# Moving the last load of wo behind the last values in the transfer queue of a decode kernel

## The chip, the cores and the metric

The kernel runs on one core of a Trainium2 chip. The metric is the device time of one execution in microseconds (us), shorter is better. Engines are called TensorE (PE in the profile; its weight loads are PEld), VectorE (DVE), ScalarE (ACT), GpSimd (POOL) and SyncE (SP, which issues nearly all transfers here). The granted clock is the share of full speed at which TensorE was allowed to run in a stretch, as the profile records it; 1.00 is full speed.

## The reference, cut to what matters

One new token passes through an attention block with cached keys and values and then a small MLP:

```python
# x: 1 x 640; 32 heads of 192; 32768 cached positions; bf16
q = layernorm(x) @ wq
p = softmax(q . k_cache * 192**-0.5)          # per head, over 32768 positions
h = x + concat(p @ v_cache) @ wo              # wo: 6144 x 640
h2 = h + relu(layernorm(h) @ w1) @ w2         # w1: 640 x 1536, w2: 1536 x 640
```

The two caches are 805 MB. All else together is some 20 MB.

## The kernel before

All loads from memory go through one queue, filled by SyncE in program order. A head's keys come in two loads (6144 KB each), its values in three. `kt` holds keys, `va` and `vb` hold values, `wo_s` holds the three rows per partition of wo that two heads need. Head 31, the last (`LAST`), is cut finer so that less work is left after its last byte: keys k0 to k5, values v0, v1, two halves `vh` and four pieces `vc`.

```python
def load(dst, src, sem, *label):
    g.do(lambda: nc.sync.dma_start(out=dst, in_=src), sem, label, by=16)
...
for h in range(LAST):
    keys(h, 0)
    vals(h, 0)
    keys(h, 1)
    for ld in ((2, 1) if h == 0 else (1, 2)):
        vals(h, ld)
    if h % 2 == 0:
        if h > 0:
            g.wait("prj", h)          # the pair before has been projected
        load(wo_s[:], wo_view[h // 2], "dwo", "wo", h // 2)
...
end_keys(0, 0, JL, "dk0")                                # k0, after waits for head 30
end_values(0, 0, JL * Dh, "dvb", "v", LAST, 0)           # v0
end_keys(1, P * JL, JL, "dke0")                          # k1
...                                                      # k2 to k5, v1, vh, vc
g.wait("PV", LAST, 3)
load(w1_s, B_w1.rearrange("(c p) n -> p c n", p=P), "dw1", "w1")
for i, (c0, c1) in enumerate(zip(W2_CUTS[:-1], W2_CUTS[1:])):    # cuts 0, 6, 9, 11, 12
    load(w2_s[:, c0:c1], B_w2.rearrange("(c p) n -> p c n", p=P)[:, c0:c1], f"dw2_{i}", "w2", i)
```

w1 and w2 go where k0 and k1 were. GpSimd passes landings on to TensorE and VectorE (`relay`), so that a wait for a key or value load reads as a wait for POOLq in the profile. TensorE and ScalarE take somewhat more than half of the keys (transposes, copies, scores as matmuls), VectorE the rest; TensorE does all values. The order of TensorE in head 31:

```python
transposes(g, h, 0); transposes(g, h, 1); scores_pe(g, h, 0)     # k0
values(g, h, 0); scores_pe(g, h, 1)
transposes(g, h, 2)                                              # k1
o_turn(g, h - 1); values(g, h, 1); scores_pe(g, h, 2)
transposes(g, h, 3); transposes(g, h, 4)                         # the latter: k2
...
project(g, h + 1)                                                # waits for the last wo
... h1 = w1 (60 matmuls), then per piece of w2:
for i, (f0, f1) in enumerate(zip(W2_CUTS[:-1], W2_CUTS[1:])):
    g.wait("w2", i)
    pe_group(g, [... w2_s[:, f, n * P:(n + 1) * P] ... for f in range(f0, f1) for n in range(DT)], ("y", i), "pe_dve")
```

The softmax here doesn't subtract the row's maximum and nothing guards it: scores larger than these inputs give would overflow.

## Time and profile before

| | before |
|---|---|
| time, first three runs | 1918.17 us median (1917.4 to 1920.89) |
| span of the profiled execution | 1915.3 us |
| bytes moved, mean rate | 825.29 MB, 431 GB/s |
| landing of k1, issue to landing | 27.7 us |

In a profile line such as those below, the first number is the start in us from the beginning of the span, the second the duration, then engine, source line, operation, what it writes and reads, and how many instructions were merged into the line. What stands in brackets is the idle time of the engine just before, and what ended it. A transfer's line in the list of issues has its size and the time from its issue to its landing. The prediction below shows the lines of before and reads them.

### The profile page before, as it was taken

To read this page: it belongs to the slowest core of one execution; us is meant where nothing else is said; L and a number is where in the kernel's file an instruction comes from. 1 tells how busy PE (TensorE), PEld (TensorE's weight loads), DVE (VectorE), ACT (ScalarE), POOL (GpSimd) and SP (SyncE) were. 2 spreads that over 40 slices of the span, in tenths; PEclk is the share of its full clock that TensorE was granted. 3 is DMA by queue.
4 is the path that set the end of the run, shared out by engine and by line. 5 is a ranking of instruction groups with operands and counts; after the bars stand their busy time and mean duration, and the time that the engine had idled before them with its cause. 6 is when DMAs were issued, how large, how long until landed. Compare 5 with 4: busy or idle time off the path is not lost.

```text
span 1915.3 us, 36109 instructions
## 1 busy us (share of the span) xinstructions
PE 1551.1 (81%) x15899; PEld 1085.0 (57%) x15899; DVE 1561.3 (82%) x731; ACT 939.5 (49%) x2000; POOL 1.0 (0%) x6
## 2 busy tenths in 40 slices
PE   7778887887878788877878877778788787877888
PEld 7555555655555555555556555556555555555555
DVE  2797787987878978789787888878798787987897
ACT  2455454554544544545545445445355454554444
POOL 0000000000000000000000000000000000000000
PEclk9888998888988889888898888898888898888988
DMA  9999999999999999999999999999999999999998
GB/s 409 430 434 433 430 435 431 435 436 433 434 431 434 435 429 431 435 432 439 434 429 435 434 431 435 434 429 437 431 434 438 431 436 429 437 431 433 431 432 367
DMA packets 29650, 825.29 MB, mean 431 GB/s; under 512 B 3131, under 2 KB 4668, under 8 KB 8124
## 3 DMA queue, kind: packets, MB, share of 16 engines
q1 hardware_dynamic: 29616, 824.98, 99.9%
q8 instruction: 15, 0.25, 0.0%
q14 instruction: 7, 0.06, 0.0%
q10 hardware_dynamic: 12, 0.00, 0.0%
HBM read 824.97 MB, written 0.00 MB: 431 GB/s over the span
## 4 chain that ended last, share of the span: by engine, by line
DVE 39%; DMA 38%; PE 15%; ACT 6%; issue 1%; DVEq 0%; POOLq 0%; SPq 0%
DMA kt<-in_A_k_cache_dram 36%; DVE sc L706 19%; DVE pr L703 18%; PE o_ps L360 7%; PE tp L379 6%; ACT kT L606 5%; DMA va<-in_A_v_cache_dram 2%; PE sp L360 1%; DVE o_pair L718 1%; ACT pA L621 1%; DVE oT L728 0%; DMA kt<-in_A_wq_dram 0%; DVE rec L711 0%; DVE rec L712 0%; DVE odd L724 0%
## 5 line engine op out<-in xcount | busy, mean ns | idle before, releaser
L703 DVE TENSOR_TENSOR pr<-kt,qb 128x2304 f32<-128x2304 bf16 (+2 forms) x257 | 756.7, 2944 | 314.8 <-POOLq L321 286.7
L606 ACT COPY kT<-tp 128x1024 bf16<-128x1024 bf16 (+1 forms) x898 | 814.3, 1017 | 272.9 <-PE tp L379 272.9
L379 PE MATMUL tp<-ident_f,kt 128*128 128x128 f32 x3456 | 588.4, 331 | 239.5 <-POOLq L342 162.9
L706 DVE TENSOR_REDUCE sc<-pr 128x12 f32<-128x2304 f32 (+2 forms) x257 | 756.1, 2942 | 8.9
L379 PEld LDWEIGHTS tp<-ident_f,kt 128*128 128x128 f32 x3456 | 482.7, 170 | 291.2 <-POOLq L342 168.7
L360 PE MATMUL o_ps<-va,pB 128*2 128x384 bf16 x1152 | 222.1, 341 | 65.0 <-POOLq L342 65.0
L360 PEld LDWEIGHTS sp<-qm,kT 128*128 128x128 bf16 x6912 | 197.2, 98 | 83.9 <-issue 42.8
L360 PE MATMUL sp<-qm,kT 128*128 128x2 bf16 x6912 | 214.5, 164 | 25.9 <-ACT pB L612 24.4
L360 PE MATMUL o_ps<-vb,pB 128*2 128x384 bf16 x1152 | 213.1, 331 | 22.9 <-ACT pA L621 22.3
L621 ACT ACTIVATE pA<-sc 128x12 bf16<-128x12 f32 (+2 forms) x257 | 58.2, 226 | 346.1 <-DVEq L65 346.1
L612 ACT ACTIVATE pB<-sp 128x20 bf16<-128x20 f32 (+2 forms) x258 | 52.4, 203 | 310.3 <-PE sp L360 310.3
L360 PEld LDWEIGHTS o_ps<-va,pB 128*2 128x2 bf16 x1152 | 94.4, 86 | 161.5 <-POOLq L342 72.4
L360 PE MATMUL o_ps<-va,pA 128*2 128x384 bf16 x896 | 172.2, 334 | 0.0
L360 PE MATMUL o_ps<-vb,pA 128*2 128x384 bf16 x896 | 166.7, 326 | 0.0
L360 PEld LDWEIGHTS o_ps<-vb,pB 128*2 128x2 bf16 x1152 | 89.9, 84 | 122.2 <-ACT pA L621 28.2
L360 PEld LDWEIGHTS o_ps<-va,pA 128*2 128x2 bf16 x896 | 77.4, 86 | 76.1 <-issue 9.6
L360 PEld LDWEIGHTS o_ps<-vb,pA 128*2 128x2 bf16 x896 | 75.2, 84 | 70.2
L612 ACT ACTIVATION_READ_ACCUMULATOR pB<-sp 128x1 f32 x258 | 55.1, 214 | 0.0
L621 ACT ACTIVATION_READ_ACCUMULATOR pA<-sc 128x1 f32 x257 | 53.1, 206 | 0.0
L360 PE MATMUL o_ps<-xn_ln,kt 128*96 128x1 bf16 (+1 forms) x316 | 22.3, 208 | 2.7 <-DMA kt<-in_A_wq_dram 2.7
L360 PEld LDWEIGHTS o_ps<-xn_ln,kt 128*96 128x96 bf16 (+1 forms) x316 | 22.1, 174 | 2.8 <-issue 2.7
L718 DVE TENSOR_SCALAR o_pair<-o_ps,rec 2x384 bf16<-2x384 f32 x32 | 19.4, 605 | 1.5 <-PE o_ps L360 0.4
(69 smaller groups left out, 186.5 us busy)
## 6 DMA issues: line engine op xcount, KB each, us to landing
kt<-in_A_k_cache_dram SPq DMA_DIRECT2D x62, 6144.0 KB, 26.8
vb<-in_A_v_cache_dram SPq DMA_DIRECT2D x63, 3072.0 KB, 20.8
va<-in_A_v_cache_dram SPq DMA_DIRECT2D x31, 6144.0 KB, 26.8
kt<-in_A_k_cache_dram SPq DMA_DIRECT2D x3, 3072.0 KB, 21.3
wo_s<-in_A_wo_dram SPq DMA_DIRECT2D x16, 480.0 KB, 19.0
kt<-in_A_wq_dram SPq DMA_DIRECT2D x4, 1536.0 KB, 10.9
va<-in_A_v_cache_dram SPq DMA_DIRECT2D x1, 3072.0 KB, 30.7
va<-in_A_v_cache_dram SPq DMA_DIRECT2D x2, 1536.0 KB, 35.5
```

Source lines behind the costliest of these rows:

```text
L360: return lambda: pe.matmul(o, lhsT=w, rhs=r, **kw)
L379: calls.append(lambda b=b, o=o: pe.transpose(out=dst[:, b, :], in_=src[:, o:o + 2 * P].bitcast(f32), identity=ident_f[:]))
L606: g.do(lambda: act.copy(out=kT[c % 2][:, b0:b0 + nb, :], in_=src[:, 0:nb, :].bitcast(bf16)), "act_pe", ("cp", h, c, k))
L612: g.do(lambda: act.activation(out=pB[c % NB][:, 0:jp], in_=sp[:, 0:jp], func=F.Exp, scale=SCALE, accum_out=dsums[:, 2 * c + 1:2 * c + 2]), ...
L621: g.do(lambda: act.activation(out=pA[c % NB][:, 0:jd], in_=sc[c % NC][:, 0:jd], func=F.Exp, scale=SCALE, accum_out=dsums[:, 2 * c:2 * c + ...
L703: g.chain(lambda: dve.tensor_tensor(out=pr[:, 0:j1 - j0, :], in0=src[:, (off + j0) * Dh:(off + j1) * Dh].rearrange("p (j d) -> p j d", d=D ...
L706: g.chain(lambda: dve.reduce_sum(out=sc[c % NC][:, j0:j1], in_=pr[:, 0:j1 - j0, :], axis=X), "dve")
L718: g.do(lambda: dve.tensor_scalar_mul(out=o_pair[:, :, 1, :], in0=o_ps[0:2, 0:2 * Dh].rearrange("q (i d) -> q i d", i=2), scalar1=rec[0:2, ...
```

## The change

The last load of wo (for heads 30 and 31) is needed only by the last projection, at the very end, but stands in the queue ahead of all keys and values of head 31. The change puts it behind the last values, so that those keys and values come sooner. The relay of head 30 no longer waits for wo, since the last projection waits for the load itself.

```diff
@@ the queue, heads 0 to 30
-            if h % 2 == 0:
+            if h % 2 == 0 and h < LAST - 1:
                 if h > 0:
                     g.wait("prj", h)
                 load(wo_s[:], wo_view[h // 2], "dwo", "wo", h // 2)
@@ the queue, after head 31's last values
+        g.wait("prj", LAST - 1)
+        load(wo_s[:], wo_view[H // 2 - 1], "dwo", "wo", H // 2 - 1)
         g.wait("PV", LAST, 3)
         load(w1_s, B_w1.rearrange("(c p) n -> p c n", p=P), "dw1", "w1")
@@ relay
-        elif label[1] % 2 == 0:
+        elif label[1] % 2 == 0 and label[1] < LAST - 1:
             g.wait("wo", label[1] // 2)
```

## The prediction

> **What bounds the kernel now.** I read the page first, parts 1, 2 and 4 (busy shares, slices, shares of the chain that ended last), because they say whether the transfers, which are all that the change moves, are the limit.
>
> ```profile
> span 1915.3 us, 36109 instructions
> ...
> DMA  9999999999999999999999999999999999999998
> GB/s 409 430 434 433 430 435 431 435 436 433 434 431 434 435 429 431 435 432 439 434 429 435 434 431 435 434 429 437 431 434 438 431 436 429 437 431 433 431 432 367
> ...
> DVE 39%; DMA 38%; PE 15%; ACT 6%; issue 1%; DVEq 0%; POOLq 0%; SPq 0%
> ```
>
> The DMA rows are full in every slice and move 431 GB/s on average, 825.29 MB in all: for most of the span the kernel is bound by streaming the caches. The change takes no byte away. All that it can win lies at the end, between the place that the last wo load leaves (ahead of head 31's keys) and the place that it takes. So next I read the tail: the issues of transfers in narrow windows, each with its time to landing, which added to the issue time in SyncE's timeline gives when each load is there.
>
> ```profile
> va<-in_A_v_cache_dram SPq DMA_DIRECT2D x1, 6144.0 KB, 26.8
> wo_s<-in_A_wo_dram SPq DMA_DIRECT2D x1, 480.0 KB, 19.0
> kt<-in_A_k_cache_dram SPq DMA_DIRECT2D x1, 3072.0 KB, 16.1
> vb<-in_A_v_cache_dram SPq DMA_DIRECT2D x1, 3072.0 KB, 20.8
> kt<-in_A_k_cache_dram SPq DMA_DIRECT2D x1, 3072.0 KB, 27.7
> ```
>
> By the timeline these were issued at 1814.71 (head 30's last values), 1823.70 (wo), 1833.85 (head 31's first keys, k0), 1836.45 (its first values, v0) and 1836.82 (k1). They land at 1841.5, 1842.7, 1849.95, 1857.25 and 1864.5. The distances are 1.2, 7.25, 7.3 and 7.25 us: one queue, one load after the other, no gap. A 3072 KB piece takes 7.27 us, so the 480 KB of wo take 480/3072 x 7.27 = 1.14 us. Everything behind wo will be there 1.14 us sooner. Then I asked whether anybody waits for it: the chain in order of time, around the landing of k1.
>
> ```profile
> 1836.82 27.69 DMA kt<-in_A_k_cache_dram
> 1864.51 0.02 issue
> 1864.54 0.03 POOLq L342
> 1864.56 0.04 issue
> 1864.61 1.86 PE tp L379 x15
> ```
>
> The chain says that the end hangs on k1, which would promise the whole 1.14 us. But a chain names only the last releaser, not how much later it was than the next one. That is in TensorE's timeline and in the waits of 1855.8 to 1864.7:
>
> ```profile
> 1841.62 3.16 PE L360 MATMUL o_ps<-va,pB 128*2 128x384 bf16 x10 [2.83 <-POOLq L342]
> ...
> 1863.71 0.75 PE L360 MATMUL sp<-qm,kT 128*128 128x2 bf16 x24
> 1864.61 1.86 PE L379 MATMUL tp<-ident_f,kt 128*128 128x128 f32 x15
> ```
>
> ```profile
> PEld tp L379 <- POOLq L342: 0.2, 1, 0.2
> ```
>
> TensorE was at head 31's second group of scores until 1864.46 and took up k1 at 1864.61. It had waited 0.15 us (its weight side 0.23, the 0.2 of the last line). It was last held up for long at 1841.62, by head 30's last values, which are issued ahead of wo in both kernels. From there to the end it works nearly without a break.
>
> **What the Trainium skill says.** "DMA: Bandwidth & Descriptors", section "Queues, rings and completion order": on each DMA engine descriptors are consumed in ring order. The trace agrees: head 30's values land at 1841.5, wo 1.2 us later, k0 7.25 us after that, though wo was issued 10 us ahead of k0. The same page, "Anatomy of one DMA": waits for semaphores are made by the issuing sequencer, the DMA engines only consume their queues. So the moved wait (for head 29's projection) costs the queue nothing: it is long over by about 1874. The same page, "Specifications", gives a fabric ceiling of 435 GB/s and an HBM limit per core of some 358; the trace has 431, so the queue is at the former and past the latter, and no order of loads makes it faster. "TensorE: Matmul & The Clock Gate", section "What's actually happening": the clock is granted by a free-running window of activity of about 3.4 us, whose phase differs from run to run. The trace agrees as far as it can: the granted clock is 0.59 in 1842 to 1846 and 0.50 in 1884 to 1888, and 1.00 in most stretches between. That is a source of scatter larger than the effect.
>
> **The change part by part.**
>
> *Removed ahead of head 31's keys:* one wait, one issue (0.33 us on SyncE, in idle time, with 10 us to the next issue) and 1.14 us of queue. GpSimd's relay for head 30 no longer waits for wo; its next relay waits for k0 anyway, 7 us later. No compute instruction changes: the order of TensorE, VectorE, ScalarE is the same line for line.
>
> *Moved sooner by 1.14 us:* k0 to k5 and all of head 31's values. Their takers:
> - k0 (1849.95 to 1848.8): VectorE takes it at 1850.10 after 1.67 us idle, so it starts 1.1 us sooner and is done with the first chunk at 1855.7 instead of 1856.84. Then it needs the denominator of head 30, which TensorE gives at 1855.84 to 1856.24, from work that the change doesn't reach. So VectorE keeps 1856.99 - 1856.35 = about 0.6 us. Its last scores end at 1900.86 and are used by 1904.40: 3 us of slack, worth nothing.
> - k1 (1864.5 to 1863.4): TensorE gains the 0.15 to 0.23 us that it had waited.
> - k2: TensorE waits 0.55 us for it, until 1872.15, but ScalarE's copies run without idle time from 1870.77 to 1888.4 and set the pace there; an earlier transpose only waits for them. Worth 0.
> - The values: v1 (1855.94 + 30.7 = 1886.6) is used at 1887.23, behind transposes; the last four pieces land at 1896 to 1901.3 and are used at 1899.75 to 1903.0. TensorE is busy without a gap from 1887.2 to 1905.5. Worth 0.
>
> *Added behind the last values:* wo lands where the values ended, at about 1901.3. It is used at 1906.87 (projection): 5.5 us of slack. w1 and w2 keep their landings, for the same bytes lie ahead of them: w1 1894.27 + 11.8 = 1906.1, used at 1908.30; the last piece of w2 at 1911.3.
>
> ```profile
> kt<-in_B_w_dram SPq DMA_DIRECT2D x1, 160.0 KB, 7.6
> ```
>
> That one is issued at about 1903.7 (1894.27 + 9.93 is the end of the five issues, less its own half microsecond), and is used by the last 5 of the 60 matmuls that run from 1910.31 to 1912.07, so at 1911.9: slack 0.6 us.
>
> *Sum:* -0.2 us at k1, carried through TensorE and ScalarE to the end, less nothing; span 1915.3 to 1915.1. With 1918.17 measured: 1918.0 us.
>
> **The rivals.**
> 1. *The keys gate the end, and the whole 1.14 us come through.* For it speaks the chain, which goes through k1. Against it the 0.15 us in front of the transposes. It can't pay in full, either: the last piece of w2 would still land at 1911.3, so the final matmuls would win at most 0.6 us. Time 1917.0 to 1917.6. In an execution with a better granted clock in 1842 to 1864, TensorE would reach k1 sooner and this would be partly true.
> 2. *wo, or w1 and w2 behind it, come late.* For it: SyncE's issues of the last pieces take long (4.65 us for four, 9.93 for five), so the queue takes only so much at once, and one more load there could delay w2's last issue, which has 0.6 us of slack. Against it: at any time past 1842.7 the same bytes have been issued and moved in both kernels, and by 1903.7 wo is gone. If it did, up to 1 us slower: 1919.2.
> 3. *The head 30 relay of wo held GpSimd and so head 31's start.* It would give something only if wo landed after k0; it lands 7.25 us ahead. 0.
>
> **Range and chances.** The rivals span 1917.0 to 1919.2; the three runs of before alone span 1917.4 to 1920.89, because of the clock and the starting phase. So the range is the scatter: 1915.6 to 1920.6. To leave 2% the time would have to move by 38 us, more than thirty times the load that moves; I give 0.005 to each side, for a disturbed run.
>
> **What would show it.** In the profile after: k1 lands about 1.1 us sooner against head 30's last values (22 instead of 23 us after them); TensorE's transposes of k1 show no wait for GpSimd and follow the scores at once; VectorE's first chunk of head 31 starts 1.1 us sooner, its second only 0.6; wo lands near 1901, over 4 us ahead of its projection; w1 and w2 land as before. The prediction is wrong if TensorE waits for wo or w2 at the end, or if a wait for keys or values of head 31 was hidden behind another releaser, so that the span falls by 0.5 us or more beyond the scatter.

## The result, and the profile after

The changed kernel took 1917.09 us (median of 4 runs, 1917.02 to 1918.77), the kernel before 1919.53 us in the runs counted with it (median of 4, 1917.4 to 1921.38). The ratio is 0.999 with a 95% interval of 0.9976 to 1.0004: the same. A ratio here is the mean time of one kernel's fast runs over the mean of the other's fast runs of the same rounds, so it is not quite the ratio of the medians.

The measured 1917.09 us lies in the predicted range, and "within 2%" was right. But the profile did not look as foretold. First the page of the changed kernel, its busy slices of the transfers and the chain that ended last: the stream is as full as before, and moves the same bytes.

```profile
DMA  9999999999999999999999999999999999999998
...
DVE 39%; DMA 39%; PE 15%; ACT 5%; issue 1%; DVEq 0%; SPq 0%; POOLq 0%
```

Then TensorE's timeline around head 31's first keys. The first line is the start of head 30's last values, the second follows its last value group, the third is the score group ahead of k1, the fourth the transposes of k1, the fifth those that begin with k2.

```profile
1841.44 1.79 PE L362 MATMUL o_ps<-va,pB 128*2 128x384 bf16 x10 [2.21 <-POOLq L344]
...
1853.98 0.40 PE L362 MATMUL mm<-dsums,ones_mat 128*128 128x20 f32 x2
...
1861.84 0.75 PE L362 MATMUL sp<-qm,kT 128*128 128x2 bf16 x24
1863.26 1.86 PE L381 MATMUL tp<-ident_f,kt 128*128 128x128 f32 x15 [0.67 <-POOLq L344]
...
1871.05 1.86 PE L381 MATMUL tp<-ident_f,kt 128*128 128x128 f32 x15 [0.78 <-POOLq L344]
```

Head 30's last values took TensorE 12.5 us here (1841.44 to 1853.98) and 14.2 us in the profile of before (1841.62 to 1855.84). The work is the same; the granted clock differed: 1.00 here from 1842 to 1846, 0.59 there. So TensorE came to k1 sooner, and although k1 now landed 1.3 us sooner (1837.25 + 25.92 = 1863.17), it still waited 0.67 us for it.

Last the end, in the chain of the changed kernel in order of time and in TensorE's timeline. Where before the chain ended in TensorE's and VectorE's own work, now it goes through a load of w2:

```profile
1894.19 0.55 SPq L232
1894.74 0.04 issue
1894.78 16.48 DMA kt<-in_B_w_dram
1911.26 0.05 issue
1911.31 0.71 PE attT L362 x15
```

```profile
1905.79 0.53 PE L362 MATMUL attT<-oT,wo_s 128*128 128x1 bf16 x15 [0.32 <-DVE oT L730]
...
1907.21 1.65 PE L362 MATMUL o_ps<-xn_ln,kt 128*128 128x1 bf16 x60
1909.31 0.94 PE L362 MATMUL attT<-h1T,kt 128*128 128x1 bf16 x30 [0.45 <-ACT h1T L678]
1910.46 0.56 PE L362 MATMUL attT<-h1T,kt 128*128 128x1 bf16 x15 [0.21 <-DMA kt<-in_B_w_dram]
1911.31 0.69 PE L362 MATMUL attT<-h1T,kt 128*128 128x1 bf16 x15 [0.29 <-DMA kt<-in_B_w_dram]
```

TensorE reached the last projection at 1905.79, 1.08 us sooner than before (1906.87), and w2's matmuls at 1909.31, 1.0 us sooner than before (1910.31):

```profile
1906.87 0.53 PE L360 MATMUL attT<-oT,wo_s 128*128 128x1 bf16 x15 [0.32 <-DVE oT L728]
...
1910.31 1.76 PE L360 MATMUL attT<-h1T,kt 128*128 128x1 bf16 x60 [0.36 <-ACT h1T L676]
```

Then it waited 0.5 us for w2, in two stops, and was done at 1912.0; before it was done at 1912.1. Both spans are 1915.3 us. So two questions were open. Is the wait for k1 worth 0.2 us, as the profile of before said, or over 1 us, as that of after suggests? And is it w2 that takes the gain back?

### The profile page after: what moved, and what is told of

It is laid out like the page before. It is cut to its first block, busy times and chain, and to the rows that moved or that the text cites. A ratio compares the mean times of both kernels' runs of the same rounds, so it can differ in the third digit from the quotient of the medians.

```text
span 1915.3 us, 36109 instructions
## 1 busy us (share of the span) xinstructions
PE 1554.4 (81%) x15899; PEld 1089.8 (57%) x15899; DVE 1561.4 (82%) x731; ACT 939.4 (49%) x2000; POOL 1.0 (0%) x6
## 4 chain that ended last, share of the span: by engine, by line
DVE 39%; DMA 39%; PE 15%; ACT 5%; issue 1%; DVEq 0%; SPq 0%; POOLq 0%
DMA kt<-in_A_k_cache_dram 35%; DVE sc L708 19%; DVE pr L705 18%; PE tp L381 7%; PE o_ps L362 7%; ACT kT L608 5%; DMA va<-in_A_v_cache_dram 2%; PE sp L362 1%; DVE o_pair L720 1%; DMA kt<-in_B_w_dram 1%; ACT pA L623 1%; DVE oT L730 0%; DMA kt<-in_A_wq_dram 0%; DVE rec L713 0%; DVE rec L714 0%
```

## The experiments

Two pairs of theories were set against each other, under these names in the expectations. On the wait for k1: **PACE**, the prediction's step (TensorE arrives together with k1, so sooner keys are worth 0.2 us), against **LOTTERY** (how long TensorE waits for k1 depends on the clock that it was granted just ahead, and the profile of before showed the slow draw). On the end: **LAST BYTE** (the end follows the last piece of w2, so the bytes ahead of it count and their order doesn't), against **KEYS** (the end follows head 31's keys).

### Both kernels again

No edit. Two more profiles, and five timed rounds.

> The kernel before, unchanged, against itself: 1917 to 1921 us, ratio 1.000. Both theories want from its profile what TensorE waits for k1 (the second keys of head 31). Theory LOTTERY (the wait for k1 depends on the granted clock just ahead of it): with full clock in 1842 to 1846 TensorE waits 1.5 to 1.8 us for k1, with a cold clock there 0.1 to 0.3 us. Theory PACE (the prediction's step: TensorE arrives with k1, so keys are worth 0.2 us): 0.1 to 0.3 us again, whatever the clock.

> The changed kernel again: ratio to before 0.999, between 0.998 and 1.001. Theory LOTTERY: with full clock ahead of k1 the last matmuls wait 0.3 to 0.6 us for w2, with a cold clock they wait for nothing; the span is 1915 to 1916 in both. Theory PACE: no wait for w2 beyond 0.1 us, the first profile's 0.5 us being chance.

The kernel before against itself: 1918.8 us median (1917.12 to 1919.02), ratio 0.9999 (0.9986 to 1.0013). The changed kernel: 1917.55 us (1916.76 to 1918.09), ratio 0.9997 (0.9983 to 1.001). The timeline of TensorE in the second profile of before, first at k1, then at k2:

```profile
1862.58 0.75 PE L360 MATMUL sp<-qm,kT 128*128 128x2 bf16 x24
1865.16 1.86 PE L379 MATMUL tp<-ident_f,kt 128*128 128x128 f32 x15 [1.83 <-POOLq L342]
...
1873.93 1.86 PE L379 MATMUL tp<-ident_f,kt 128*128 128x128 f32 x15 [1.77 <-POOLq L342]
```

The same kernel now waits 1.83 us for k1, where its first profile showed 0.15. PACE is refuted. Every later profile with the usual loads ahead of k1 fits LOTTERY, sorted by the mean granted clock from 1841.5 to 1856, the stretch in which TensorE does head 30's last values:

| kernel (names of the experiments) | granted clock | wait for k1, us |
|---|---|---|
| before; before_w2rows | 0.88; 0.88 | 0.15; 0.15 |
| before_again; before_nomlp | 1.00; 1.00 | 1.83; 1.83 |
| after_x_nomlp; after_w2rows; after_w2pairs | 0.88; 0.88; 0.88 | none |
| after; after_again; after_nomlp; after_nowo; after_x | 1.00 (all five) | 0.67; 0.67; 0.68; 0.66; 0.66 |

At full clock the change takes 1.83 - 0.67 = 1.16 us from this wait, which is the load's own 1.14 us. With the slower clock the wait is 0.15 us before and none after, so there the sooner keys are worth what the prediction said. The sizes agree: head 30's last values took 14.2 us in all profiles of the slower clock and 12.5 us in all of the full one, and this difference of 1.7 us is that of the two waits before (1.83 - 0.15). No run sets the clock, so this is an agreement of twelve profiles and not an experiment on the clock.

How much of the 1.16 us reaches the end is less clear. From the start of head 30's last values to the last projection, TensorE took 65.25 and 65.41 us in the two profiles of before's order with the slower clock, and 64.98 to 65.12 us in the three of after's: 0.1 to 0.4 us, near the predicted 0.2. With the full clock it was 66.27 and 67.44 us against 63.82 to 65.68 us in five. So before's order came later to the end with the faster clock than with the slower one, and more than the wait for k1 differs between these profiles.

The second profile of after repeats the end of the first: three stops for w2.

```profile
1909.65 0.94 PE L362 MATMUL attT<-h1T,kt 128*128 128x1 bf16 x30 [0.50 <-DMA kt<-in_B_w_dram]
1910.80 0.73 PE L362 MATMUL attT<-h1T,kt 128*128 128x1 bf16 x15 [0.21 <-DMA kt<-in_B_w_dram]
1911.70 0.69 PE L362 MATMUL attT<-h1T,kt 128*128 128x1 bf16 x15 [0.17 <-DMA kt<-in_B_w_dram]
```

Of the first 0.50 us some 0.36 is the usual idle time there (the wait for ScalarE's h1T in the profile of before), so w2 cost about 0.5 us in all, as in the first profile. The second profile of before has no stop for w2, and its matmuls began at 1911.89.

### Without w1 and w2

```diff
-        load(w1_s, ...)                 # and the loop over the pieces of w2
-        g.wait("w1")                    # and g.wait("w2", i)
```

Done to both kernels; the result is wrong, as the MLP reads old keys.

> The kernel before without the loads of w1 and w2 (wrong result on purpose: the last matmuls read old keys in their place), so that nothing lands behind the last values. LOTTERY: k1 sets the end, which w2 already met within 0.6 us: 0 to 0.6 us under before. PACE: the same as before within 0.3 us.

> The changed kernel without the loads of w1 and w2 (wrong result on purpose). LOTTERY: the sooner keys now come through to the end: 0.9 to 1.2 us under the other kernel without these loads. PACE: 0.2 us under it.

Measured: 1919.59 us (1917.03 to 1920.8) and 1916.81 us (1915.09 to 1919.04), ratios to before 1.0004 (0.999 to 1.0017) and 0.9993 (0.9979 to 1.0006). The difference of the ratios is 0.0011 or 2 us, in the direction of LOTTERY, but the intervals overlap and the first of the two was not under before at all. By times alone this is inconclusive: the effect of one wo load is smaller than the scatter of single runs. So the next experiment moved more.

### The same move, 5.8 times as large, with and without loads behind it

Two more loads of 1.18 MB each (into a part of the key buffer that is free at that time, used by nobody) stand beside wo: ahead of head 31's keys in the kernel before, behind the last values in the changed kernel.

```diff
@@ before_x: ahead of head 31's keys (k1, which overwrites them, waits for them)
+        for t, o in enumerate((64 * Dh, 104 * Dh)):
+            load(kt[0][:, o:o + 24 * Dh], rows(k_hd, 0, 0, JL)[:, t * 24 * Dh:(t + 1) * 24 * Dh], f"dxt{t}", "xt", t)
         end_keys(0, 0, JL, "dk0")
...
+        g.wait("xt", 0)
+        g.wait("xt", 1)
         end_keys(1, P * JL, JL, "dke0")
@@ after_x: behind wo, ahead of w1
         g.wait("PV", LAST, 3)
+        for t, o in enumerate((40 * Dh, 104 * Dh)):
+            load(kt[0][:, o:o + 24 * Dh], ...)
         load(w1_s, ...)
```

Each was run with w1 and w2, and without them (wrong result).

> The kernel before with two more loads of 1.18 MB each (into a free part of the key buffer, used by nobody) beside wo, ahead of head 31's keys: 4.8 times what the change moves. At 7.27 us for 3072 KB they take 5.45 us of queue. Theory LAST BYTE (the end follows the last piece of w2, so only the bytes ahead of that count): 5.0 to 5.7 us over before. Theory KEYS (the end follows k1): 5.0 to 5.7 us over before as well.

> The changed kernel with the same two loads behind wo, that is behind the last values and ahead of w1 and w2. LAST BYTE: 4.5 to 5.7 us over before, the same as the other kernel with these loads within 1 us, though the keys come 6.6 us sooner in it; TensorE waits for w1 and w2. KEYS: as the changed kernel without them, 0 to 1 us under before.

> Extra loads ahead of the keys, and no loads of w1 and w2 (wrong result on purpose). Both theories: the keys gate the end, 4.5 to 5.7 us over before.

> Extra loads behind the last values, and no loads of w1 and w2 behind them (wrong result on purpose). Both theories: as the changed kernel without w1 and w2, 0 to 1.5 us under before, so 5 to 6.5 us under the kernel with the extra loads ahead of the keys. Together with the pair that has w1 and w2: LAST BYTE wants a difference by position of 0 +- 1 us with them and of 5 to 6.5 us without them; KEYS wants 5 to 6.5 us in both.

| | extra loads ahead of the keys | behind the last values | difference of medians |
|---|---|---|---|
| with w1 and w2 behind | 1922.7 us (1922.42 to 1923.11) | 1922.84 us (1921.99 to 1923.7) | 0.1 us |
| without | 1923.4 us (1921.61 to 1925.66) | 1916.36 us (1915.82 to 1917.12) | 7.0 us |

This is LAST BYTE: where w1 and w2 come behind, it makes no difference where 2.9 MB of loads (the two and wo) stand, and where nothing comes behind, it makes 7 us. (Queue time of the two loads and wo: 5.45 + 1.14 = 6.6 us; expected were 5 to 6.5.) KEYS had asked for 5 to 6.5 us in both rows. The timelines of TensorE show what becomes of the sooner keys. Extra loads ahead of the keys, with w1 and w2:

```profile
1912.08 0.53 PE L364 MATMUL attT<-oT,wo_s 128*128 128x1 bf16 x15 [0.32 <-DVE oT L732]
1913.51 1.65 PE L364 MATMUL o_ps<-xn_ln,kt 128*128 128x1 bf16 x60
1915.52 1.76 PE L364 MATMUL attT<-h1T,kt 128*128 128x1 bf16 x60 [0.36 <-ACT h1T L680]
```

Extra loads behind the last values, with w1 and w2:

```profile
1907.88 0.53 PE L364 MATMUL attT<-oT,wo_s 128*128 128x1 bf16 x15 [0.32 <-DVE oT L732]
1913.37 1.74 PE L364 MATMUL o_ps<-xn_ln,kt 128*128 128x1 bf16 x60 [3.69 <-DMA kt<-in_B_w_dram]
1915.92 0.94 PE L364 MATMUL attT<-h1T,kt 128*128 128x1 bf16 x30 [0.81 <-DMA kt<-in_B_w_dram]
1917.07 0.56 PE L364 MATMUL attT<-h1T,kt 128*128 128x1 bf16 x15 [0.20 <-DMA kt<-in_B_w_dram]
1917.86 0.70 PE L364 MATMUL attT<-h1T,kt 128*128 128x1 bf16 x15 [0.23 <-DMA kt<-in_B_w_dram]
```

TensorE is 4.2 us sooner at the last projection, and gives 3.69 + 0.81 + 0.20 + 0.23 = 4.93 us back waiting for w1 and w2 (of the 0.81, 0.36 is the usual idle time).

That k1 waits for the extra loads, which the other arrangement doesn't ask of it, is not what delayed it: TensorE took up k1 28.5 us after head 30's last values with the extra loads ahead, against 23.0 us in before, and the difference is the queue time of the extra loads (5.45 us). Without w1 and w2 the profiled run (the slowest of its four) had 29.8 us; this slip of 1.4 us, unexplained, is part of that kernel's scatter.

Against before, all four came out lower than expected. By their ratios, with w1 and w2, the extra bytes cost 3.8 us ahead of the keys (1.002, interval 1.0003 to 1.0036; expected 5.0 to 5.7) and 3.5 us behind the values (1.0018, 1.0001 to 1.0035; expected 4.5 to 5.7). Without w1 and w2 it was 3.8 us over before (1.002, 1.0003 to 1.0036; expected 4.5 to 5.7) and 2.9 us under it (0.9985, 0.9968 to 1.0002; expected 0 to 1.5). Each interval reaches the expected values; the before runs of that call alone ran from 1916.81 to 1920.75. The comparisons in the table don't go through before.

### Without the last load of wo

```diff
-        g.wait("prj", LAST - 1)
-        load(wo_s[:], wo_view[H // 2 - 1], "dwo", "wo", H // 2 - 1)
-            g.wait("wo", H // 2 - 1)
```

> The changed kernel without the last wo load at all (wrong result on purpose: the last projection uses the rows of the pair before). Keys as in the changed kernel, w1 and w2 1.14 us sooner than in it. LAST BYTE: 0.4 to 0.9 us under the changed kernel, and no wait for w2. KEYS: the same as the changed kernel.

Measured 1915.89 us (1915.55 to 1916.84), ratio 0.9989 (0.9975 to 1.0003). That is 1.7 us under the median of the changed kernel's own repeat on the same chip, more than the 0.4 to 0.9 expected; by its profile there is no wait for w2 left, as LAST BYTE wants, and TensorE is at w2's matmuls at 1908.64. This fits LAST BYTE: taking 480 KB away from the tail shows more than moving them within it. But the two intervals overlap (the repeat's is 0.9983 to 1.001), so by times it is suggested, not shown. (Its result is wrong, yet it passes the comparison with the reference: the part of the last two heads is below the tolerance. That comparison alone would not have found a wo load that came too late.)

### w2 in larger pieces

If w2 takes the gain back, a w2 that lands sooner should keep it. Its rows of 1280 bytes make 1536 pieces. Letting each partition take consecutive rows makes fewer and longer ones, but w1's columns must then be read with a stride.

```diff
-            load(w2_s[:, c0:c1], B_w2.rearrange("(c p) n -> p c n", p=P)[:, c0:c1], f"dw2_{i}", "w2", i)
+            load(w2_s[:, c0:c1], B_w2.rearrange("(p c) n -> p c n", p=P)[:, c0:c1], f"dw2_{i}", "w2", i)
...
-        w1_s[:, c, f * P:(f + 1) * P]
+        w1_s[:, c, f:Dff:FT]            # stride 12
```

> The changed kernel with w2 loaded so that each partition takes consecutive rows (pieces of 7680, 3840, 2560 and 1280 bytes in place of rows of 1280), and w1's columns read with a stride of 12 to match. LAST BYTE: w2's pieces land up to 1 us sooner, the last matmuls wait less for them, 0.3 to 0.9 us under the changed kernel. KEYS: the same as the changed kernel.

> The kernel before with the same w2 layout. Both theories: within 0.3 us of before, because there w2 is in time; so with this layout the change is worth 0.6 to 1.1 us (LAST BYTE) against 0.2 us (the prediction's step at k1).

Measured 1919.7 us (1918.91 to 1920.7), ratio 1.0008, on the changed kernel, and 1919.49 us (1918.89 to 1922.86), ratio 1.001, on the kernel before: the first was expected 0.3 to 0.9 us under the changed kernel, the second within 0.3 us of before, and both medians came out over. The groups of the changed kernel with this layout from 1907 to 1914 show why; the columns are busy time and mean ns of one.

```profile
L362 PE MATMUL o_ps<-xn_ln,kt 128*128 128x1 bf16 x60 | 3.8, 200 | 0.0
L362 PEld LDWEIGHTS o_ps<-xn_ln,kt 128*128 128x128 bf16 x60 | 3.7, 160 | 0.1
```

The hidden layer's 60 matmuls took 3.8 us, 2.1 us more than the 1.65 us of the unstrided version: a weight load with stride 12 took 160 ns in place of 96 (164 in place of 96 on the kernel before). The side effect was larger than the effect, so this says nothing on w2's landing by its time. A milder form has pieces of two rows and a stride of 2:

```diff
+            load(w2_s[:, c0:c1].rearrange("p (g t) n -> p g t n", t=2),
+                 B_w2.rearrange("(g p t) n -> p g t n", p=P, t=2)[:, c0 // 2:c1 // 2], f"dw2_{i}", "w2", i)
...
+        w1_s[:, c, f // 2 * 2 * P + f % 2:f // 2 * 2 * P + 2 * P:2]
+    W2_CUTS = (0, FT // 2, FT - 4, FT - 2, FT)
```

> The changed kernel with w2 in pieces of two rows (2560 bytes in place of 1280, half as many), w1's columns read with a stride of 2 in place of 12. If the stride cost the 2.1 us of the version with stride 12, the 60 matmuls of the hidden layer are back near 1.65 us (under 1.9). LAST BYTE: w2 waits shrink by 0.2 to 0.6 us, time 0 to 0.6 us under the changed kernel's 1917.1 to 1917.6. KEYS: the same as the changed kernel.

Measured 1916.79 us (1916.51 to 1917.35), ratio 0.9991 (0.9978 to 1.0005), the lowest of the correct kernels. Its groups and TensorE's timeline at the end:

```profile
L363 PEld LDWEIGHTS o_ps<-xn_ln,kt 128*128 128x128 bf16 x60 | 1.6, 97 | 0.1
```

```profile
1907.86 1.65 PE L363 MATMUL o_ps<-xn_ln,kt 128*128 128x1 bf16 x60
1909.87 1.76 PE L363 MATMUL attT<-h1T,kt 128*128 128x1 bf16 x60 [0.36 <-ACT h1T L679]
```

With stride 2 the weight loads cost nothing extra, and w2 is no longer waited for. But this profile fell on the slow draw of the clock (0.88 in the table above), in which TensorE comes late anyway, and the time's interval includes the changed kernel. That the pieces are what removed the wait is likely, not shown.

## Why the prediction was right, and where it was not

**The stream bounds the kernel, and the loads land in order.** Right. Against head 30's last values k1 landed 21.8 us later in place of 23.0 (foretold: 22 in place of 23); wo landed at 1873.23 + 28.2 = 1901.4 (foretold: near 1901), 4.4 us ahead of its use at 1905.79.

**What the keys are worth: 0.2 us.** This step failed, in its generality: the path to the end it had right for the execution that it read, the wait for k1 it had wrong for others. It read the slack of one execution (0.15 us at k1) as a property of the kernel. It is 0.15 us with the slow draw of the clock and 1.83 us with the fast one, in the same kernel. Of the fast draw's wait the change takes 1.16 us. The prediction had named this, as the first rival's case of a better granted clock, but gave it no weight. Its mark for the profile after, that the transposes of k1 show no wait and follow the scores at once, was wrong: 0.67 us were left.

**w2's last piece caps the gain at 0.6 us.** That was put down to the first rival, and it carried the result. The prediction's main line had no wait for w2, and named one as a sign that it was wrong ("if TensorE waits for wo or w2 at the end"); that sign came true. In both profiles of after TensorE stops for w2; in the enlarged version the order of the loads is worth 0.1 us with w1 and w2 behind it and 7.0 us without.

**w1 and w2 keep their landings.** Nearly. The same bytes are ahead of them, but w1 landed at 1893.19 + 13.6 = 1906.8 in place of 1906.1. Counted from the start of head 30's last values that is 65.4 us in place of 64.5, and 65.7 in the second profile of before, so it lies within what one kernel shows; why is open. Part of the wait for w2 may come from this and not from TensorE's sooner arrival. The stream as a whole is not steady to a microsecond: from k1 to k2, both 3072 KB, took some 7.5 us in the first profile of before and 8.8 us in the second (k1 taken at 1865.16, k2 at 1873.93, both waited for). No experiment here tells why.

**VectorE gains 1.1 us at k0 and keeps 0.6.** It kept 1.0 us (1856.95 in place of 1857.94 for its second chunk), for head 30's denominator came sooner with the clock. Worth nothing, as said.

**The sum and the range.** 1918.0 us was foretold and 1917.09 measured; the range came from the scatter, and rightly. It was so wide that it held every rival (1917.0 to 1919.2), and the measured median lies in that of the first, so the number speaks for no mechanism; that it came out right in spite of the two steps above is due to the width of the range and the small size of the moved load. Over all calls, the kernel before ran 43 times with a mean of 1918.6 us (1916.6 to 1921.4), the changed kernel 9 times with a mean of 1917.5 us (1916.8 to 1918.8). These come from several chips and are not a paired comparison, so a gain near 1 us is suggested, not shown. The narrower spread of the changed kernel would fit an end that is tied to w2's landing rather than to the clock; that too is argued only.

## What to carry to other kernels

In this stream, full from start to end, moving a load backwards bought time only up to the next load that the end waits for: look for the last transfer's consumer and its slack before looking at what comes sooner. A slack that a single profile shows beside a clock-dependent engine is one draw; take a second profile before building a sum on it. Where an effect is smaller than the scatter, enlarge it several times and cross it with the suspected cap, as the four runs with extra loads did here.

## What the Trainium skill lacked or had wrong

- "TensorE: Matmul & The Clock Gate", section "LDWEIGHTS (loading the stationary operand)", makes the time of a weight load a matter of the number of columns alone. The runs show that their stride matters too, which that section does not say: 96 ns for 128 adjacent bf16 columns, 97 ns with a stride of 2 (4 bytes), 160 ns with a stride of 12 (24 bytes).
- "DMA: Bandwidth & Descriptors", section "Specifications", lists an HBM limit of some 358 GB/s per core without saying that both cores of a pair must be streaming for it to hold; the section "Bandwidth" of the same page does say so. The one core of this program held 431 GB/s over 1915 us here.
- The same page, section "Queues, rings and completion order", gives the order within a queue; no page says how steady its landings are. With a full queue the time from one 3072 KB landing to the next was 7.3 to 8.8 us in these profiles.
